# Two pairs' sums over heads and the zero words of the masks, moved from GpSimd to VectorE

## The chip, the cores and the metric

The kernel runs on one core of one Trainium2 chip. The metric is device time in microseconds (us) of the whole program. Before the change three runs gave 1026.31 (median), 1023.31 and 1027.18. The core has TensorE (matrix products), VectorE and ScalarE (elementwise work, ScalarE also the exponentials), GpSimd (elementwise work and indirect transfers), and queues from which transfers are issued; here SyncE's and GpSimd's are used. In the profile they are PE, DVE, ACT, POOL and SP. Each engine takes its instructions strictly in the order in which they were written into its queue.

## The reference

Eight batches of eight heads, 576 tokens, 64 numbers per head. Keys and values are averaged over groups of 8 tokens, so each head has 72 pooled keys. Attention over these gives one row of 512 numbers for each of 4608 tokens. Each row then goes through a mixture of eight experts:

```
logits = x @ w_gate
noisy  = logits + log1p(exp(x @ w_noise)) * noise
top2   = the two largest of the 8 noisy logits, with softmax weights
out    = sum over the two: weight * (relu(x @ w1[e]) @ w2[e])
```

with w1[e] 512x1024 and w2[e] 1024x512.

## The kernel before

**Attention.** Two batches form a pair, and there are four pairs, 0 to 3. A pair is worked through in nine chunks of 128 tokens (`ci` 0 to 8), 36 chunks in all. For each chunk TensorE transposes queries, makes scores (`qk`, lines 365 and 375), ScalarE exponentiates against a maximum from VectorE (lines 380 and 382), TensorE transposes again (`et`) and multiplies with the values (`av`, line 408). The values carry 16 more columns per head, the products of v with the two gate matrices, so that `av` also gives each head's share of the gate and noise logits. VectorE divides by the softmax sum and writes the attention rows (`xr`, line 419) and these shares (`lg`, line 421, a 128x128 product per chunk: 8 heads by 16 columns). The rows go to memory (`x_dram`).

**Routing.** `route(pr, ...)` is a generator, one for each pair. First it adds `lg` over the eight heads, in three adds that halve the number of heads each (lines 508 and 509), once for chunks 0 to 7 and once for chunk 8; in the kernel before, GpSimd does this. Line 516 on VectorE is the first reader of these sums. A chain of short VectorE and ScalarE steps on 128x72 numbers follows (softplus, the two maxima, a mask `mb` of the chosen experts at line 566). The mask has eight more columns of zeros behind its nine chunks, which the memset at line 565 writes, on GpSimd; there is one `mb` buffer for all pairs. TensorE then counts, with triangular and all-ones matrices, how many tokens chose each expert before a given one (`rk`, the rank matmuls at line 593). From rank and expert VectorE works out the place of each record (`pos`) and its words (`rec`, up to line 634).

**Record writes and the list `scq`.** Each pair has 18 record writes (9 chunks, two choices), indirect transfers on GpSimd's queue (line 637), put on a list. Behind those of pair 1 come the load of the first records of expert 0 (line 678, on GpSimd's queue) and the gathers of the first four tiles of rows (`fetch(groups[0])`, line 705, four indirect transfers on GpSimd's queue); behind pair 2's and pair 3's the same for further tiles. The program takes entries from the list a few at a time, at fixed places in each chunk: `advance(n, m)` runs `n` steps of the routing generator and then takes `m` entries. In pairs 2 and 3 a chunk takes three or four. `quiet` is 0 in chunks in which nothing is taken: in the kernel before, chunk 0 of every pair, and chunk 8 of every pair but the last. Each write also waits for an instruction of the chunk that takes it (`pace`).

**Experts.** Expert 0's tokens come in three groups. Group 0 needs only records of pairs 0 and 1, group 1 those of pairs 0 to 2, group 2 all. Stage 1 multiplies by w1 in eight blocks of 128 hidden features; each block takes twelve matmuls for a group of 512 columns (line 1016), goes into one of eight banks, and is evicted by ScalarE (`hh`, line 1027) and VectorE (`hl`, line 1028). Stage 2 multiplies by w2 (lines 1127 and 1093). Weights are split in two parts on ScalarE and VectorE (lines 480 and 481). The routing of pair 3 is driven from the first blocks of stage 1 of group 0 (`hook1`): its first sums are called in chunk 8 of pair 3, everything else after blocks 0 to 3, and the rank matmuls of pair 3 come in the program after the fourth block.

**Order.** The program's order gives priorities; a planner then writes each engine's queue from these and from its own estimates of durations, so that an instruction may stand earlier or later in its queue than the program has it.

Of the kernel before, what the change touches and what calls it, by code (L numbers as in the profile page):

```python
# [19 lines left out]
def kernel(  # L20
# [12 lines left out]
    nc = tc.nc  # L33
# [12 lines left out]
    NP = B // 2  # L46
    NCH = 9
# [286 lines left out]
    def qtr(u, half, hp=None):  # L334
        kind, pr, b, jp = u
        if half == 0:
            QTT[u] = ap_.tile([P, H, P], F32, tag="qT", name=f"qT{pr}_{b}_{jp}", bufs=2)
        elif kind == "R":
            return
        qT = QTT[u]  # L340
        qp = ps2.tile([P, 4, P], F32, tag="one", name=f"qp{pr}_{b}_{jp}_{half}", bufs=2)
        for i in range(4):
            if kind == "R":
                src = QR[pr][:, 2 * i:2 * i + 2]
            else:
                src = QT[b][:, half * 4 + i, 2 * jp:2 * jp + 2]
            nc.tensor.transpose(qp[:, i], src.rearrange("p a d -> p (a d)"), ident)  # L347
        with tc.high_priority(offset=HP if hp is None else hp):
            nc.scalar.copy(qT[:, half * 4:half * 4 + 4], qp)
# [35 lines left out]
    def et(u, jj):  # L385
        kind, pr, b, jp = u
        nm = f"{pr}_{b}_{jp}_{jj}"
        ex = EX[u][:, jj]
        eT = ap_.tile([P, NEB, P], F32, tag="eT", name=f"eT{nm}", bufs=2)
        for n0, n1 in EG:  # L390
            ep = ps2.tile([P, 512], F32, tag="one", name=f"ep{nm}_{n0}", bufs=2)
            for n in range(n0, n1):
                nc.tensor.transpose(ep[:BST, (n - n0) * P:(n - n0 + 1) * P], ex[:, ES[n]:ES[n] + BST], ident)  # L393
            with tc.high_priority(offset=HP):
                (nc.vector.tensor_copy if n0 and EV >> jj & 1 else nc.scalar.copy)(eT[:BST, n0:n1].rearrange("p n t -> p (n t)"), ep[:BST, :(n1 - n0) * P])  # L395
        return eT
# [50 lines left out]
    def wload():  # L447
        if not pieces:
            return
        e, i, h = pieces.pop(0)  # L450
        st = wp.tile([P, DF], F32, tag="wst", name=f"wst{e}_{i}_{h}", bufs=WS)
        if i < 2:
            src = moe_w1[e].rearrange("(p c) f -> p c f", p=P)[:, 2 * i + h]
            dst = st
        else:
            r0 = (i - 2) * 4 * P + h * 2 * P
            src = moe_w2[e, r0:r0 + 2 * P, :].rearrange("(c p) f -> p c f", p=P)
            dst = st.rearrange("p (c f) -> p c f", c=2)
        nc.sync.dma_start(dst, src)
        staged.append(st)  # L460
# [26 lines left out]
    def drain(g):  # L487
        for _ in g:
            pass
# [4 lines left out]
    def route(pr, c0, c1, lg, psum):  # L494
        n = c1 - c0
        k_ = [0]

        def t(*shape, dt=F32):
            k_[0] += 1
            ci = shape.index(NCH)  # L500
            r = rp.tile([P] + list(shape), dt, tag=f"rt{k_[0]}", name=f"rt{pr}_{c0}_{k_[0]}")
            return r[:, :n] if ci == 0 else r[:, :, :n]

        V = nc.vector
        L = t(NCH, 2 * E)
        for a, b in ((c0, c1 - 1), (c1 - 1, c1)):
            for h in (4, 2):
                nc.gpsimd.tensor_add(lg[:, a:b, :h], lg[:, a:b, :h], lg[:, a:b, h:2 * h])  # L508
            nc.gpsimd.tensor_add(L[:, a - c0:b - c0], lg[:, a:b, 0], lg[:, a:b, 1])
            if b < c1:  # L510
                yield
                if pr < NP - 1:
                    yield
# [48 lines left out]
            mxs.append(mx)  # L562
            ms.append(m)
        mb = rp.tile([P, NCH + 1, E], BF16, tag="mb", name=f"mb{pr}_{c0}")
        nc.gpsimd.memset(mb[:, n:], 0.0)
        V.tensor_add(mb[:, :n], ms[0], ms[1])
        rec = rp.tile([P, NCH, 2, RW], I32, tag="rec", name=f"rec{pr}_{c0}", bufs=4)

# [175 lines left out]
    def rows_of(grp, psum):  # L744
        e, t0, nt = grp
        xh = wp.tile([P, NDB, 4 * P], F32R, tag="q", name=f"xh{e}_{t0}", bufs=2)
        xl = wp.tile([P, NDB, 4 * P], F32R, tag="q", name=f"xl{e}_{t0}", bufs=2)
        XT[grp] = (xh, xl)
        for t in range(nt):
            xg = XG.pop((e, t0 + t))  # L750
            if e == 0:
                xp = psum(f"xp{t0 + t}").rearrange("p (b c) -> p b c", b=NDB)
                xv = xg.rearrange("p (c b) -> p b c", b=NDB)
                for db in range(NDB):
                    nc.tensor.transpose(xp[:, db], xv[:, db], ident)
                nr = 2 if t0 + t == 9 else 4
                xT = xp.rearrange("p b (r j) -> p b r j", j=32)[:, :, :nr]
            else:
                nr = 2 if t0 + t == 9 else 4
                xt = pools[0].tile([P, 4, NDB, 32], F32, tag="xt", name=f"xt{e}_{t0 + t}", bufs=2)  # L760
                nc.vector.transpose(xt[:, :nr], xg[:, :nr * P].rearrange("p (r i b) -> p r b i", i=32, b=NDB))
                xT = xt.rearrange("p r b j -> p b r j")[:, :, :nr]
            cs = slice(t * P, t * P + nr * 32)
            xhv = xh[:, :, cs].rearrange("p b (r j) -> p b r j", j=32)
            xlv = xl[:, :, cs].rearrange("p b (r j) -> p b r j", j=32)
            SP_[0] = (nc.scalar.copy(xhv, xT), nc.vector.tensor_sub(xlv, xT, xhv.bitcast(F32)))  # L766
            yield
# [13 lines left out]
    def advance(n, m):  # L781
        for _ in range(n):
            while gens:
                try:
                    next(gens[0])
                    break
                except StopIteration:
                    gens.pop(0)
        for _ in range(min(m, len(scq))):
            scq.pop(0)()  # L790
# [84 lines left out]
    for i, (ui, u, jj) in enumerate(chunks):  # L875
        pr, ci = divmod(i, NCH)
        if ci == 0:
            lgs[pr] = (rp if pr % 2 else ap_).tile([P, NCH, H, 2 * E], F32, tag="lg", name=f"lg{pr}")
        single = u[0] == "R"
        has = ui + 1 < NU  # L880
        if single:
            order = OR
        else:
            order = OD[jj]
        eT = None
        quiet = 0 if ci == 0 or ci == NCH - 1 and pr < NP - 1 else 1

        def bgs():
            for f in bg.get(i, ()):
                f()  # L890

        def adv():
            pace[0] = lastx[0]
            advance(STEPS[pr], 2 * quiet if pr >= NP // 2 else quiet)

        for o in order + ("" if "b" in order else "b") + ("" if "x" in order else "x"):
            if o == "v" and i == 0:
                drain(pg[0])
            if o == "b":
                bgs()  # L900
            elif o == "x":
                adv()
            elif o == "e":
                eT = et(u, jj)
            elif o == "v":
                if due:
                    due.pop()()
                if ci == NCH - 1 and pr < NP - 1:
                    gens.append(route(pr, 0, NCH, lgs[pr], one))
                elif ci == NCH - 1:  # L910
                    rt = route(pr, 0, NCH, lgs[pr], lambda nm: mone(nm))
                    next(rt)
                due.append(lambda u=u, jj=jj, ci=ci, eT=eT, lg=lgs[pr]: av(u, jj, ci, eT, lg))
            elif o in "012":
                if has:
                    qk(units[ui + 1], int(o))
                    if pr and (o == "0" or not single):
                        pace[0] = lasta[0]
                        advance(0, quiet)
            elif ui + 2 < NU:  # L920
                qtr(units[ui + 2], "qr".index(o))
        if i == 24:
            for _ in range(WS):
                wload()
        if i == 33:
            splits = rows_of(groups[0], one)
        if pr == 3 and ci:
            with tc.issue_after(lastl[0].ins), tc.issue_after(lasta[0].ins):
                next(first[0], None) if ci < 5 else next(first[1], None)
        if ci == 4 and pr >= HS:  # L930
            gens.append(route(pr, 0, 5, lgs[pr], one))
# [206 lines left out]
    def mone(name):  # L1138
        return bank()
# [174 lines left out]
```

## Time and profile before

| | |
|---|---|
| median of 3 runs | 1026.31 us |
| profiled execution, its own time | 1026.68 us |
| its span in the trace | 1024.9 us |
| PE busy | 989.9 us, 97% |
| DVE busy | 546.1 us, 53% |
| ACT busy | 343.8 us, 34% |
| POOL busy | 377.5 us, 37% |
| granted TensorE clock, mean | 0.986 of full |

The time of the profiled execution is the span plus what lies around it, 1.8 us. The page cuts the span into 40 slices of 25.6 us and gives a busy digit for each, in tenths (9 is 90% or more); PEclk is the granted clock of TensorE in the same way, where 1.00 of a window is 2.4 GHz and 0.50 is 1.2 GHz. A busy PE is not a PE at its peak. A "releaser" (after `<-`) is the instruction whose end let a waiting instruction start.

### The profile page before, as it was taken

The page shows a single profiled execution, that of the slowest core. Times are in us where ns is not written, and L with a number is a line of the kernel's source. Part 1 is how long each engine was busy: PE and PEld are TensorE (multiplying, and loading weights), DVE is VectorE, ACT ScalarE, POOL GpSimd, SP SyncE. Part 2 cuts the span into 40 slices and gives each one's busy share as a digit, 9 for nine tenths or more (in the row PEclk, how much of TensorE's full clock was granted, in tenths as well). Part 3 has the DMA queues.
Part 4 walks back from the last instruction along what each step waited for, and adds up shares of the span by engine and source line. Part 5 has one row for each costly group of instructions (what it writes and reads, how often), then busy time and mean ns, then how long its engine had stood idle before and what let it go on. Part 6 is the DMA issues. An engine that isn't in the chain of part 4 may idle for free.

```text
span 1024.9 us, 16467 instructions
## 1 busy us (share of the span) xinstructions
PE 989.9 (97%) x5832; PEld 888.6 (87%) x5832; DVE 546.1 (53%) x1261; ACT 343.8 (34%) x857; POOL 377.5 (37%) x433
## 2 busy tenths in 40 slices
PE   7999997979999999999999999999999999999996
PEld 6898896869998888898988898989888988898995
DVE  5799886583344454644464446444644455356341
ACT  4787785451213212411142124211421232123120
POOL 3023574846300442145115421551154215422514
PEclk8999998989999999999999999999999999999998
DMA  9989883344607765676267736772678358744623
GB/s 252 250 250 273 227 263 112 115 146 98 208 15 218 215 180 148 199 238 206 74 188 219 239 114 201 249 217 70 182 235 256 93 161 256 245 144 135 211 87 136
DMA packets 136006, 187.61 MB, mean 183 GB/s; under 512 B 29123, under 2 KB 84052, under 8 KB 135898
## 3 DMA queue, kind: packets, MB, share of 16 engines
q1 hardware_dynamic: 110458, 119.09, 40.5%
q0 software_dynamic: 25440, 67.05, 21.0%
q8 instruction: 72, 1.18, 0.5%
q14 instruction: 36, 0.29, 0.1%
HBM read 123.31 MB, written 70.74 MB: 189 GB/s over the span
## 4 chain that ended last, share of the span: by engine, by line
PE 87%; POOL 3%; issue 3%; ACT 2%; DMA 2%; DVE 1%; SPq 1%; POOLq 0%; ACTq 0%; DVEq 0%
PE bank L1016 37%; PE bank L1127 28%; PE bank L1093 10%; PE a L408 4%; PE s L375 2%; PE ep L393 2%; POOL rec_dram L637 1%; PE qp L347 1%; DMA v<-in_v_dram 1%; ACT ex L382 1%; ACT eT L395 1%; POOL lg L508 1%; POOL out_dram L1072 1%; PE s L365 1%; DMA rec_dram<-rec,pos 0%
## 5 line engine op out<-in xcount | busy, mean ns | idle before, releaser
L1016 PE MATMUL bank<-xh,w 128*128 128x512 f32 (+6 forms) x1536 | 391.2, 339 | 0.0
L1016 PEld LDWEIGHTS bank<-xh,w 128*128 128x128 f32 x1536 | 271.1, 189 | 20.6
L1127 PE MATMUL bank<-w,hh 128*128 128x512 f32 x880 | 271.3, 389 | 0.0
L1016 PE MATMUL bank<-xl,w 128*128 128x512 f32 (+6 forms) x768 | 260.3, 339 | 0.0
L1027 ACT ACTIVATE hh<-bank 128x512 fp32r<-128x512 f32 (+4 forms) x192 | 97.3, 508 | 460.0 <-PE bank L1016 435.7
L1028 DVE SCALAR_TENSOR_TENSOR hl<-bank,hh 128x512 fp32r<-128x512 f32 (+4 forms) x192 | 111.0, 579 | 242.2 <-ACT hh L1027 242.2
L1127 PEld LDWEIGHTS bank<-w,hh 128*128 128x128 f32 x880 | 164.9, 188 | 33.8
L1127 PE MATMUL bank<-w,hl 128*128 128x512 f32 x440 | 171.4, 389 | 0.0
L1016 PEld LDWEIGHTS bank<-xl,w 128*128 128x128 f32 x768 | 145.0, 189 | 10.4
L1064 DVE SCALAR_TENSOR_TENSOR pv<-bank,raw,pv 128x128 f32<-128x128 f32 x196 | 55.5, 342 | 109.1 <-PE bank L1127 62.4
L1068 POOL DMA_DIRECT2D slot_dram<-yt x17 | 9.8, 575 | 270.4 <-DVE yt L1064 218.4
L1093 PE MATMUL bank<-hh,w 128*128 128x240 f32 (+3 forms) x512 | 103.3, 298 | 3.1 <-ACT xh L766 1.8
L1127 PEld LDWEIGHTS bank<-w,hl 128*128 128x128 f32 x440 | 82.6, 188 | 17.2
L637 POOL DMA_INDIRECT rec_dram<-rec,pos x72 | 78.3, 1088 | 48.8 <-issue 14.2
L1048 POOL DMA_INDIRECT pv<-slot_dram,raw x70 | 68.1, 973 | 65.4 <-DMA slot_dram<-ys 33.3
L481 DVE TENSOR_TENSOR w<-wst,w 128x512 fp32r<-128x512 f32 x128 | 82.6, 681 | 10.5 <-ACT w L480 10.5
L1093 PEld LDWEIGHTS bank<-hh,w 128*128 128x128 f32 x512 | 82.5, 189 | 3.6 <-ACT xh L766 2.0
L480 ACT CAST w<-wst 128x512 fp32r<-128x512 f32 x128 | 72.8, 619 | 25.4 <-DMA wst<-in_moe_w_dram 25.2
L714 POOL DMA_INDIRECT row<-x_dram,raw x70 | 70.4, 1006 | 21.4 <-issue 19.8
L1068 POOL DMA_DIRECT2D slot_dram<-pv x55 | 31.7, 577 | 123.8 <-DVE pv L1064 97.1
L1093 PE MATMUL bank<-hl,w 128*128 128x320 f32 (+3 forms) x256 | 75.8, 296 | 0.0
L382 ACT ACTIVATE ex<-s,mx 128x72 f32<-128x72 f32 x288 | 70.6, 344 | 9.9 <-DVE mx L380 9.6
(162 smaller groups left out, 1029.6 us busy)
## 6 DMA issues: line engine op xcount, KB each, us to landing
wst<-in_moe_w_dram SPq DMA_DIRECT2D x64, 512.0 KB
via<-row SPq DMA_DIRECT2D x266, 64.0 KB
xg<-via SPq DMA_DIRECT2D x63, 256.0 KB
slot_dram<-pv POOLq DMA_DIRECT2D x55, 256.0 KB, 4.0
x_dram<-xr SPq DMA_DIRECT2D x16, 512.0 KB
q<-in_q_dram SPq DMA_DIRECT2D x7, 1024.0 KB
k<-in_k_dram SPq DMA_DIRECT2D x6, 896.0 KB
v<-in_v_dram SPq DMA_DIRECT2D x12, 432.0 KB
```

Of the source, the lines that this page charges most:

```text
L382: lasta[0] = nc.scalar.activation(ex[:, jj, EPOS[h] * G:(EPOS[h] + 1) * G], sv[:, i], AF.Exp, bias=mx[:, i:i + 1])
L480: nc.scalar.copy(hv, sv)
L481: nc.vector.tensor_sub(lv, sv, hv.bitcast(F32))
L637: s = nc.gpsimd.indirect_dma_start(out=rec_dram[:, :], out_offset=bass.IndirectOffsetOnAxis(ap=pos[:, i, c:c + 1], axis=0), in_=rec[:, c, ...
L714: turn_of("pool", lambda: nc.gpsimd.indirect_dma_start(out=row[:32 * nr], out_offset=None, in_=x_dram[:, :], in_offset=bass.IndirectOffset ...
L1016: nc.tensor.matmul(part(ph), w1s(e, a, db, f), part(xs[b][:, db]), start=(i == 0), stop=(i == 3 * NDB - 1))
L1027: act = nc.scalar.activation(hh[:, :n], ph[:, :n], AF.Relu)
L1028: last = nc.vector.scalar_tensor_tensor(hl[:, :n], ph[:, :n], 0.0, hh[:, :n].bitcast(F32), op0=OP.max, op1=OP.subtract)
L1048: turn_of("pool", lambda: nc.gpsimd.indirect_dma_start(out=pv[:np_], out_offset=None, in_=slot_dram[:P + e * CAP, :], in_offset=bass.Indir ...
L1064: nc.vector.scalar_tensor_tensor(r_, y_, wc, pv[:plain] if plain else r_, op0=OP.mult, op1=OP.add)
L1093: nc.tensor.matmul(part(py), w2s(e, b, f)[:, mb * P:(mb + 1) * P], part(hs[f][a]), start=(i == 0), stop=(i == 3 * NFB - 1))
L1127: mm = nc.tensor.matmul(py, hs[f][a][:, cs], w2s(e, b, f), start=(i == 0), stop=(i == 3 * NFB - 1))
```

## The change

The adds over heads use VectorE for pairs 2 and 3 and stay on GpSimd for pairs 0 and 1. The memset of the mask's zero words is on VectorE for all pairs. `quiet` is 1 now in chunk 8 of pair 2 and in chunk 0 of pair 3, so entries of the list are taken there too. (`NP` is 4, `NCH` is 9.)

```diff
         for a, b in ((c0, c1 - 1), (c1 - 1, c1)):
+            eng = nc.gpsimd if pr < NP // 2 else V
             for h in (4, 2):
-                nc.gpsimd.tensor_add(lg[:, a:b, :h], lg[:, a:b, :h], lg[:, a:b, h:2 * h])
-            nc.gpsimd.tensor_add(L[:, a - c0:b - c0], lg[:, a:b, 0], lg[:, a:b, 1])
+                eng.tensor_add(lg[:, a:b, :h], lg[:, a:b, :h], lg[:, a:b, h:2 * h])
+            eng.tensor_add(L[:, a - c0:b - c0], lg[:, a:b, 0], lg[:, a:b, 1])
...
         mb = rp.tile([P, NCH + 1, E], BF16, tag="mb", name=f"mb{pr}_{c0}")
-        nc.gpsimd.memset(mb[:, n:], 0.0)
+        V.memset(mb[:, n:], 0.0)
...
-        quiet = 0 if ci == 0 or ci == NCH - 1 and pr < NP - 1 else 1
+        quiet = 0 if ci == 0 and pr <= NP // 2 or ci == NCH - 1 and pr < NP // 2 else 1
```

## Rows read from the trace of the kernel before

**Rows 1.** The page: busy times; granted clock in 40 slices, in tenths.

```profile
PE 989.9 (97%) x5832; PEld 888.6 (87%) x5832; DVE 546.1 (53%) x1261; ACT 343.8 (34%) x857; POOL 377.5 (37%) x433
...
PEclk8999998989999999999999999999999999999998
```

**Rows 2.** Waits of PE: waiter, releaser, total us, times, longest us.

```profile
PE bank L593 <- DVE mb L566: 6.9, 1, 6.9
PE s L365 <- ACT ex L382: 5.9, 1, 5.9
PE kT L298 <- DVE ks L239: 2.3, 2, 1.2
```

**Rows 3.** Windows: length; PE, PEld, DVE, ACT, POOL busy (count); PEclk, DMA share, GB/s.

```profile
140.00:151.50 11.50, 11.50 (x97) 11.11 (x95) 10.31 (x22) 10.19 (x36) 9.14 (x8) 1.00 0.86 257
...
153.40:159.30 5.90, 0.02 (x2) 0.02 (x2) 1.18 (x4) 0.91 (x6) 4.15 (x7) 0.74 0.17 53
159.30:166.00 6.70, 6.70 (x37) 5.65 (x38) 3.63 (x14) 3.17 (x12) 2.96 (x4) 0.50 0.03 3
...
185.00:192.00 7.00, 6.42 (x52) 5.91 (x50) 6.64 (x16) 5.84 (x14) 5.47 (x6) 1.00 0.60 169
...
203.40:210.40 7.00, 0.07 (x3) 0.07 (x3) 5.20 (x24) 2.68 (x9) 3.29 (x7) 0.78 0.00 0
210.40:214.40 4.00, 4.00 (x19) 3.27 (x20) 4.00 (x11) 2.59 (x6) 0.70 (x2) 0.52 0.20 35
```

**Rows 4.** Timeline of POOL, end of pair 2: start, duration, instruction, [idle before <-releaser].

```profile
153.60 0.97 POOL L637 DMA_INDIRECT rec_dram<-rec,pos  x1 [0.30 <-issue]
154.59 2.06 POOL L508 TENSOR_TENSOR lg<-lg 128x512 f32<-128x512 f32 x2
```

**Rows 5.** Timeline of DVE across the turn from pair 2 to 3.

```profile
150.43 0.28 DVE L421 TENSOR_TENSOR lg<-a,rd 128x128 f32<-128x128 f32 x1
...
158.12 0.23 DVE L516 SCALAR_TENSOR_TENSOR rt<-rt 128x72 f32<-128x72 f32 x1 [6.46 <-POOL rt L509]
...
159.41 0.28 DVE L421 TENSOR_TENSOR lg<-a,rd 128x128 f32<-128x128 f32 x1
...
166.21 0.28 DVE L421 TENSOR_TENSOR lg<-a,rd 128x128 f32<-128x128 f32 x1
...
169.90 0.28 DVE L421 TENSOR_TENSOR lg<-a,rd 128x128 f32<-128x128 f32 x1
```

**Rows 6.** Timeline of DVE at the end of attention.

```profile
193.57 0.28 DVE L421 TENSOR_TENSOR lg<-a,rd 128x128 f32<-128x128 f32 x1
203.80 0.23 DVE L516 SCALAR_TENSOR_TENSOR rt<-rt 128x72 f32<-128x72 f32 x1 [9.96 <-POOL rt L509]
```

**Rows 7.** Timeline of PE at the same place.

```profile
192.28 0.48 PE L1016 MATMUL bank<-xh,w 128*128 128x512 f32 x1
...
210.36 0.23 PE L593 MATMUL bank<-mb,before 128*128 128x80 bf16 x1 [6.93 <-DVE mb L566]
```

**Rows 8.** Groups of DVE, 100 to 215 us: count, busy us, mean ns, idle before.

```profile
L481 DVE TENSOR_TENSOR w<-wst,w 128x512 fp32r<-128x512 f32 x12 | 8.0, 683 | 0.0
...
L584 DVE TENSOR_TENSOR rec<-rec,rt 128x9 f32<-128x9 f32 x3 | 0.5, 166 | 0.0
...
L1201 DVE TENSOR_TENSOR gt<-cnt,thr 128x216 f32<-128x216 f32 x1 | 0.4, 374 | 0.0
```

**Rows 9.** Timelines of DVE and POOL: an add, and a record write beside it.

```profile
146.22 1.75 DVE L233 TENSOR_TENSOR v<-v 112x1536 f32<-112x1536 f32 x1
...
147.05 1.75 POOL L637 DMA_INDIRECT rec_dram<-rec,pos  x1 [0.30 <-DMA rec_dram<-rec,pos]
```

**Rows 10.** Waits of POOL: the memset of the mask.

```profile
POOL mb L565 <- PE rk L593: 13.4, 2, 10.7
```

**Rows 11.** Timeline of POOL and the critical chain: last gather, transposes of group 2.

```profile
254.43 0.95 POOL L705 DMA_INDIRECT xg<-x_dram,raw  x1 [0.30 <-issue]
...
263.27 1.92 PE bank L755 x16
```

## The prediction, made before the result was known

> **What bounds the kernel now.** I read the page first. TensorE is busy in 97% of the span, and its granted clock is below full in three of the forty slices: the first, the seventh (about 154 to 179 us) and the ninth (205 to 231) [rows 1]. So the kernel is bound by TensorE except where it stands still, and what a change on other engines can give is the standing still and what follows from it. The list of TensorE's waits names two long ones and after them nothing above 2.3 us: 6.9 us before the rank matmuls at line 593, and 5.9 us before the score matmuls at line 365 [rows 2]. The windows put a price on each: idle from 153.4 to 159.3 and then 6.7 us at half clock (1.2 instead of 2.4 GHz) with TensorE busy throughout; idle from 203.4 to 210.4 and then 4.0 us at a mean of 0.52 [rows 3]. These are the two slow slices.
>
> Then I asked the two in-order queues what stood at their heads. The sums over heads of pair 2 stand in GpSimd's queue behind a run of record writes of pair 1: the last write starts at 153.60, the first add at 154.59 [rows 4]. VectorE's line 516, the first reader of the sums, stands idle 6.46 us for them and starts at 158.12; behind it in VectorE's queue is the softmax work of the next chunk, whose `lg` product comes only at 159.41, nearly nine microseconds after that of the chunk before (150.43) [rows 5]. That starves ScalarE's exponentials, and they starve TensorE. At the end of attention it is the same: the last chunk's `lg` is written at 193.57, but line 516 starts at 203.80, and the row says that it waited 9.96 us for GpSimd [rows 6]. The rank matmuls, six and a half microseconds of short VectorE and ScalarE steps later, come at 210.36, while TensorE, which began stage 1 at 192.28, had run out of the four hidden blocks (128 hidden features, twelve matmuls each) in front of them at 203.4 [rows 3, 7].
>
> **The change part by part.** *Sums of pairs 2 and 3 on VectorE.* Six adds per pair move: 512, 256 and 128 elements for chunks 0 to 7, and 64, 32 and 16 for chunk 8. VectorE's price for a 128x512 add of two SBUF operands is 0.68 us (line 481); 256 elements lie between the 0.37 of 216 elements and that 0.68, I take 0.42, near the row of 216; 128 elements are 0.28 (`lg` rows); 64 to 16 elements lie between 0.17 (9 elements) and 0.28, I take 0.2 each with a few hundredths between dependent steps [rows 5, 8]. First part 1.4 us, second part 0.7, together 2.1 per pair. They depend only on VectorE's own `lg` products, so nothing in front of line 516 waits for another engine any more.
>
> *First stall.* The steps from chunk to chunk by the `lg` starts are 8.98 and 6.80 us across and after the stall, and 3.69 for the next one [rows 5]. Without stall and half clock I give the two steps 3.7 each, plus the whole 2.1 of the sums, because VectorE was busy 10.31 of 11.5 us just before and offers no hole for them [rows 3]: 9.5 instead of 15.8, a gain of 6.3. The bounds: 8.4 if the sums hide, and nothing if other work fills the hole (rival C).
>
> *Second stall.* It costs 7.0 us idle and 1.9 us of the 4.0 at half clock, 8.9 in all [rows 3]. Afterwards the chain starts at the end of the last `lg` (193.85), takes up to 2.1 for the sums and the same 6.56 from line 516 to the rank matmuls [rows 6, 7]: 202.5, against TensorE's arrival at 203.4. Two more evictions of hidden blocks (0.68 each, the same shape as line 481) may be written into the chain, which makes it 203.9. So at most half a microsecond of the stall is left, and I count no half clock behind so short a wait. Against that, the first part of the sums falls into a stretch where VectorE is busy 6.64 of 7.0 us and must still split the rows that the first hidden block needs [rows 3], so the start of stage 1 slips by up to 1.4. Gain 8.9 - 1.4 - 0.5 = 7.0; bounds 8.9 and nothing.
>
> *A rule that would take some of it back.* Beside VectorE's 1.75 us add of 112x1536 at 146.22, a record write that normally takes 0.97 took 1.75, while the add kept its usual time [rows 9]. The Trainium skill (SBUF — State Buffer, SBUF: two separate sides) says that VectorE with two SBUF inputs and a GpSimd operation share one pair of ports where GpSimd reads SBUF, and that whichever starts first holds it for the whole instruction while the other is blocked. By that rule a record write in progress could also hold up each of the three large adds for up to 0.97 us, which at the end of attention would leave a stall of 2 to 3 us more, and the sum would be about 1016. The row shows only the write giving way, so I leave this out of the sum.
>
> *The zero words of the masks on VectorE.* Four memsets. The trace has none of this size on VectorE; a 9-element operation there takes 0.17 us [rows 8], which I take as the upper end, the lower end is nothing, and I count 0.1 each, 0.2 on the path. GpSimd's were beside its queue of writes and freed nothing that TensorE waited for. Where the memset stands in VectorE's order is a different matter (rival D).
>
> *Chunks no longer kept free.* Chunk 8 of pair 2 and chunk 0 of pair 3 now take items from the list: the last two record writes of pair 1, the load of its records and the four gathers of the first rows come there instead of two chunks later. These are seven or so GpSimd issues of about 1 us. They sit on GpSimd's queue alone (this load is not on SP's), what is queued behind them is no longer the sums, and the record writes of pair 2 are put on the list only in chunk 3 of pair 3. I count nothing; it is hidden under TensorE's work, and the rows are needed only at the end of attention. Each write also waits for a marker of the chunk that issues it; that wait now has only other writes behind it.
>
> *What is late next.* From the rank matmuls on, the record writes of pair 3 and the gathers of the next groups hang on the same chain as the ranks, so they come earlier by about as much as TensorE does. The tightest place: the last gather of group 2 of expert 0 starts at 254.43, TensorE transposes its rows at 263.27 [rows 11]; after some 5 us for issue and landing, 4 us of margin stay. TensorE's own list has only waits of 2.3 us or less behind the two.
>
> **Sum.** 1026.68 (the profiled execution; 1024.9 of it is the span) - 6.3 - 7.0 + 0.2 = 1013.6. The profiled execution lies 0.37 above the median of the runs, so I forecast 1013. If everything hides: 1026.3 - 8.4 - 8.9 = 1009.
>
> **Rivals.** *B, one stall stays.* The order inside each queue is written by a planner from its own estimates. If it now writes the rank matmuls ahead of some hidden blocks (after the first, TensorE would be there near 195, the ranks at 202.5), TensorE stands as long as before and only the first stall is gained: 1026.3 - 6.3 = 1020. If the first stall is replaced instead: 1019. For it: the end of attention has less than a microsecond of slack. Against it: the rank matmuls stand in the program after the fourth block, and there they stood before.
>
> *C, no change.* VectorE, nearly full before both stalls, becomes what TensorE waits for, and the 2.1 us per pair come on top of work that had moved into the hole: 1026. Against it: VectorE's and ScalarE's idle time in the first hole is idle for the sums alone, and little is pulled ahead in an in-order queue.
>
> *D, slower.* The memset of a pair's mask may not overwrite what the rank matmuls of the pair before still read. On GpSimd it stood 13.4 us for them in two of the four cases, once 10.7 [rows 10], and nobody minded. If it stands as early in VectorE's queue, VectorE stops in the middle of attention, with the maxima and products of the next chunk behind it, and TensorE runs dry as it did at 153: 13.4 us, and about 5 us for two spells of half clock [rows 3], together 18.4 against the gain of 13.3, so 1026.3 + 5.1 = 1031. It decides as soon as these waits with their clock cost exceed 13.3 us. Against it: VectorE has its own wait for the same matmuls (the running count), and a planner that puts the memset where the ranks are done would put it behind that.
>
> **How the numbers follow.** Forecast 0.68 (own range 1009 to 1017), B 0.16, C 0.06, D 0.10. A difference under 0.5%, 5.1 us, can hardly be told from none. Faster by more than that: all of the forecast and three quarters of B, 0.80. Within: the rest of B, C and two fifths of D, 0.14. Slower: the rest of D, 0.06. The range of 1009 to 1021 holds the forecast and B and leaves out C and D.
>
> **What would show it.** Right: no 5.9 and no 6.9 in TensorE's list of waits; line 516 without a wait for GpSimd in pairs 2 and 3; the granted clock full from 154 to 231; the `lg` steps around chunk 26 near 4 to 6 us; the rank matmuls within a microsecond after the fourth hidden block. Wrong: a memset of `mb` on VectorE with microseconds of idle time before it and TensorE as releaser (D); the rank matmuls after fewer than four blocks (B); hidden blocks or transposes of group 1 or 2 waiting for gathered rows.

## The result, and the profile after

The changed kernel takes 1008.55 us (median of 4 runs, 1006.87 to 1008.85), the kernel before 1026.12: a ratio of 0.983 with a 95% interval of 0.9807 to 0.9852. A later comparison on another chip gave 1008.38 against 1025.54, 0.9831 (0.981 to 0.9852). The forecast was 1013, with a range of 1009 to 1021: the direction and the mechanism were right, the gain was 17.6 us where 13.3 had been worked out, and the time lies half a microsecond below the range. The profiled execution took 1008.4 us, its span is 1006.6.

The page of the changed kernel (as rows 1):

```profile
PE 983.0 (98%) x5832; PEld 882.3 (88%) x5832; DVE 549.7 (55%) x1277; ACT 344.4 (34%) x857; POOL 370.6 (37%) x417
...
PEclk8999999999999999999999999999999999999999
```

Only the first slice is below full now. TensorE's waits, longest first (as rows 2): both long ones are gone, and nothing has taken their place.

```profile
PE kT L298 <- DVE ks L239: 2.4, 2, 1.3
PE s L375 <- ACT ex L382: 1.9, 2, 1.4
PE vTp L317 <- DVE vs L239: 1.5, 1, 1.5
```

VectorE at the turn from pair 2 to pair 3 (as rows 5; lines below 507 keep their numbers, later ones are one higher, so the adds are 509 and 510 and their first reader is 517):

```profile
144.35 0.28 DVE L421 TENSOR_TENSOR lg<-a,rd 128x128 f32<-128x128 f32 x1
145.06 0.61 DVE L380 TENSOR_REDUCE mx<-s 128x6 f32<-128x432 f32 x1 [0.43 <-PE s L375]
145.59 0.68 DVE L509 TENSOR_TENSOR lg<-lg 128x512 f32<-128x512 f32 x1
...
146.58 0.41 DVE L509 TENSOR_TENSOR lg<-lg 128x256 f32<-128x256 f32 x1
...
147.84 0.28 DVE L421 TENSOR_TENSOR lg<-a,rd 128x128 f32<-128x128 f32 x1
...
148.56 1.75 DVE L233 TENSOR_TENSOR v<-v 112x1536 f32<-112x1536 f32 x1
...
151.03 0.95 DVE L233 TENSOR_TENSOR v<-v 112x768 f32<-112x768 f32 x1
151.90 0.23 DVE L517 SCALAR_TENSOR_TENSOR rt<-rt 128x72 f32<-128x72 f32 x1
...
153.27 0.28 DVE L421 TENSOR_TENSOR lg<-a,rd 128x128 f32<-128x128 f32 x1
...
156.60 0.28 DVE L421 TENSOR_TENSOR lg<-a,rd 128x128 f32<-128x128 f32 x1
```

Line 517 waits for nobody. The three steps between the `lg` products from 144.35 to 156.60 take 12.25 us. In the kernel before the same three go from 144.98 over 150.43 and 159.41 to 166.21 [rows 5; the first is from the same view]: 21.23. So 9.0 us come from here.

```profile
144.98 0.28 DVE L421 TENSOR_TENSOR lg<-a,rd 128x128 f32<-128x128 f32 x1
```

Note the two large `v` adds (2.7 us, pooling for a later batch): before, they stood ahead of the product at 150.43 (the larger one is in rows 9); the planner has put the sums there and the `v` adds behind the product.

TensorE's own windows say what the 9.0 us consist of (columns as in rows 3). First the kernel before: the three steps one by one, then the stretch from the product of chunk 7 of pair 2 to that of the last chunk but one. Then the changed kernel: the three steps together, and the same long stretch.

```profile
144.98:150.43 5.45, 5.45 (x47) 5.31 (x47) 4.68 (x9) 4.64 (x15) 4.54 (x4) 1.00 0.90 247
150.43:159.41 8.98, 3.07 (x33) 2.47 (x33) 2.10 (x8) 2.91 (x15) 6.40 (x10) 0.82 0.45 170
159.41:166.21 6.80, 6.80 (x38) 5.75 (x39) 3.73 (x15) 3.27 (x11) 3.17 (x4) 0.50 0.03 3
144.98:190.78 45.80, 38.98 (x309) 35.12 (x309) 30.99 (x113) 30.68 (x102) 26.21 (x30) 0.89 0.50 155
```

```profile
144.35:156.60 12.25, 12.20 (x119) 11.31 (x119) 10.77 (x33) 11.05 (x39) 9.81 (x9) 1.00 0.68 233
144.35:181.12 36.77, 35.60 (x309) 32.02 (x309) 32.49 (x121) 30.83 (x102) 23.25 (x23) 1.00 0.60 192
```

The long stretch holds 309 matmuls in both. TensorE is idle in it for 1.17 us instead of 6.82, and busy with the same work for 35.60 instead of 38.98: 5.65 us of idle time and 3.4 us of half clock are gone. VectorE is busy for 1.5 us more (32.49 instead of 30.99).

The end of attention, VectorE first (as rows 6), then TensorE (as rows 7):

```profile
184.91 0.28 DVE L421 TENSOR_TENSOR lg<-a,rd 128x128 f32<-128x128 f32 x1
185.23 0.45 DVE L509 TENSOR_TENSOR lg<-lg 128x64 f32<-128x64 f32 x2
185.72 0.18 DVE L510 TENSOR_TENSOR rt<-lg 128x16 f32<-128x16 f32 x1
185.93 0.26 DVE L517 SCALAR_TENSOR_TENSOR rt<-rt 128x72 f32<-128x72 f32 x1
...
192.72 0.22 DVE L567 TENSOR_TENSOR mb<-rt,rt 128x72 bf16<-128x72 f32 x1
```

```profile
182.62 0.47 PE L1017 MATMUL bank<-xh,w 128*128 128x512 f32 x1
183.48 0.50 PE L1017 MATMUL bank<-xl,w 128*128 128x512 f32 x1 [0.39 <-DVE xl L767]
...
194.31 0.21 PE L594 MATMUL bank<-mb,before 128*128 128x80 bf16 x1
```

The mask is ready at 192.94, TensorE comes to the rank matmuls 1.4 us later and does not wait; the large adds of the sums stand between the two splits that the first block needs, and cost it a wait of 0.39. On the critical chain the transposes of group 2 start 17.76 us earlier than in rows 11:

```profile
245.51 1.92 PE bank L756 x16
```

The product of the last chunk but one stands at 181.12 where it stood at 190.78, 9.66 earlier; so the end of attention gives the other 8.1. Of the 9.66, 0.6 were there already in chunk 6 of pair 2 (140.71 against 141.34); runs of other kernels that change nothing up to there stood up to 0.95 earlier too, so I do not count it to the change.

### The profile page after: what moved, and what is told of

Read it like the earlier page. It is cut to its first block, busy times and chain, and to the rows that moved or that the text cites. A ratio compares the mean times of both kernels' runs of the same rounds, so it can differ in the third digit from the quotient of the medians.

```text
span 1006.6 us, 16461 instructions
## 1 busy us (share of the span) xinstructions
PE 983.0 (98%) x5832; PEld 882.3 (88%) x5832; DVE 549.7 (55%) x1277; ACT 344.4 (34%) x857; POOL 370.6 (37%) x417
## 4 chain that ended last, share of the span: by engine, by line
PE 90%; ACT 3%; issue 2%; DMA 2%; POOL 1%; DVE 1%; SPq 1%; POOLq 0%; ACTq 0%; DVEq 0%
PE bank L1017 39%; PE bank L1128 28%; PE bank L1094 10%; PE a L408 4%; PE s L375 3%; PE ep L393 2%; PE qp L347 1%; DMA v<-in_v_dram 1%; ACT ex L382 1%; ACT eT L395 1%; POOL out_dram L1073 1%; PE vr L325 0%; PE kT L298 0%; PE s L365 0%; POOL slot_dram L1069 0%
## 5 line engine op out<-in xcount | busy, mean ns | idle before, releaser
L481 DVE TENSOR_TENSOR w<-wst,w 128x512 fp32r<-128x512 f32 x128 | 82.7, 684 | 11.9 <-ACT w L480 11.9
```

Of the source, the lines that this page charges most:

```text
L481: nc.vector.tensor_sub(lv, sv, hv.bitcast(F32))
```

## The experiments

Eighteen runs, in the order of the questions. Each is compared with the kernel before on its own chip.

**Which pair gives what.** The sums of one pair alone on VectorE, memset and kept-free chunks as before; the edit of the kernel before, cut to the lines changed:

```diff
+            eng = V if pr == 2 else nc.gpsimd
...
-                nc.gpsimd.tensor_add(lg[:, a:b, :h], lg[:, a:b, :h], lg[:, a:b, h:2 * h])
-            nc.gpsimd.tensor_add(L[:, a - c0:b - c0], lg[:, a:b, 0], lg[:, a:b, 1])
+                eng.tensor_add(lg[:, a:b, :h], lg[:, a:b, :h], lg[:, a:b, h:2 * h])
+            eng.tensor_add(L[:, a - c0:b - c0], lg[:, a:b, 0], lg[:, a:b, 1])
```

> Only the sums of pair 2 on VectorE. Where the kernel before takes 1026 to 1028 (its two stalls are there): theory 9 us less, 1018, the 5.9 us wait gone and the 6.9 us wait left; rival (the prediction's 6.3 us) 1021. Where the kernel before takes 1048 as on two other chips (TensorE stands elsewhere and the two stalls are not there): no difference.

Measured: 1016.49 against 1026.03, ratio 0.9913 (0.9889 to 0.9936): 9.5 us less. Its waits of TensorE begin with the one that was left:

```profile
PE bank L594 <- DVE mb L567: 6.9, 1, 6.9
PE vTp L317 <- DVE vs L239: 2.7, 1, 2.7
```

And with `pr == 3`:

> Only the sums of pair 3 on VectorE. Where the kernel before takes 1026 to 1028: theory 8 us less, 1019, the 6.9 us wait gone and the 5.9 us wait left; rival (the ranks still come late while the first stall is there) 1023 or more. Where it takes 1048: no difference.

Measured: 1017.51 against 1026.03, ratio 0.9919 (0.9901 to 0.9937): 8.5 us less, and the other wait left:

```profile
PE s L365 <- ACT ex L382: 5.9, 1, 5.9
```

The two add up to 18.1 us against 17.6 of the whole. So each stall belongs to its own pair's sums, they do not hang together, and the first is worth some 9 us and not 6.3.

**Queue order or the speed of the adds.** The sums stay on GpSimd, but chunk 7 of pair 2 takes no record writes either, so four fewer stand in front of them:

```diff
-        quiet = 0 if ci == 0 or ci == NCH - 1 and pr < NP - 1 else 1
+        quiet = 0 if ci == 0 or ci == NCH - 1 and pr < NP - 1 or pr == 2 and ci == NCH - 2 else 1
```

> Kernel before with chunk 7 of pair 2 kept free of record writes too, sums on GpSimd. Where the kernel before takes 1026 to 1028: theory (the writes in front make the sums late) the first stall goes without VectorE, 1018 to 1020; rival (GpSimd's slower adds are the matter) 1025 to 1027. Where it takes 1048: no difference.

Measured: 1021.08 against 1026.03, ratio 0.9956 (0.9939 to 0.9972): 5.0 us less. That is a little over the theory's 1018 to 1020 and well under the rival's 1025 to 1027. Line 516 waits 0.82 us instead of 6.46, so the writes in front were what made the sums late, and the rival falls. But nearly half of the 9 us is missing. TensorE's row at line 365, two windows at and behind it, and the long stretch (product of chunk 7 of pair 2 to that of the last chunk but one) show where (columns as in rows 3):

```profile
153.23 0.71 PE L365 MATMUL s<-kbd,qT 64*64 64x72 f32 x14 [0.76 <-ACT ex L382]
```

```profile
153.00:154.00 1.00, 0.77 (x15) 0.69 (x16) 1.00 (x4) 1.00 (x5) 0.54 (x1) 1.00 0.09 37
154.00:161.00 7.00, 7.00 (x30) 6.04 (x31) 4.46 (x19) 3.27 (x10) 4.79 (x5) 0.51 0.13 43
144.07:184.65 40.58, 38.90 (x309) 35.06 (x309) 31.92 (x112) 30.84 (x102) 25.48 (x29) 0.92 0.51 167
```

TensorE waits 0.76 us, once, and its clock is nevertheless at 1.2 GHz from 154 to about 161, with TensorE busy all the time. Over the long stretch its idle time is 1.68 us, nearly as little as in the changed kernel (1.17), but it is busy for 38.90 us, as in the kernel before (38.98), where the changed kernel needs 35.60. So this run takes away the idle part of the stall, and the 3.3 us of half clock stay. Why the clock falls here is not shown: a longer wait at nearly the same place, in the run with extra adds below, leaves it full. The end of attention in this kernel is unchanged in kind (a wait of 8.1 us before the rank matmuls).

**The freed chunks alone**, sums and memset on GpSimd:

```diff
-        quiet = 0 if ci == 0 or ci == NCH - 1 and pr < NP - 1 else 1
+        quiet = 0 if ci == 0 and pr <= NP // 2 or ci == NCH - 1 and pr < NP // 2 else 1
```

> Only the chunks freed for record writes, sums and memset on GpSimd. Where the kernel before takes 1026 to 1028: theory (queue order on GpSimd makes the sums late) the first stall grows by 1.3 to 8 us, 1028 to 1035; rival (the freed chunks count nothing whoever does the sums) 1026 to 1027. Where the kernel before takes 1048: no difference.

Measured: 1030.0 against 1025.54, ratio 1.0038 (1.0021 to 1.0055): slower, as the queue order has it. GpSimd's timeline shows the sums of chunk 8 behind the load and the four gathers, and the list of TensorE's waits a stall of 12.7 us:

```profile
155.85 0.96 POOL L637 DMA_INDIRECT rec_dram<-rec,pos  x1 [0.30 <-issue]
156.83 2.07 POOL L508 TENSOR_TENSOR lg<-lg 128x512 f32<-128x512 f32 x2
...
165.62 0.96 POOL L705 DMA_INDIRECT xg<-x_dram,raw  x1 [0.31 <-issue]
166.60 0.66 POOL L508 TENSOR_TENSOR lg<-lg 128x64 f32<-128x64 f32 x2
```

```profile
PE ep L393 <- ACT qT L349: 13.4, 3, 12.7
```

**The same edits taken back one at a time from the changed kernel.** First the chunks kept free as before:

> Changed kernel with chunk 8 of pair 2 and chunk 0 of pair 3 kept free of record writes as before. Theory (freeing them counts nothing once the sums are off GpSimd): 1008 to 1009. Rival (the freed chunks gave the 2 to 3 us by which the first stall's gain exceeded the forecast): 1011.

Measured: 1008.19 against 1027.76 (0.9813, 0.9791 to 0.9834). Then the memset on GpSimd as before:

> Changed kernel with the zero words of the masks written by GpSimd as before. Theory (the memset counts nothing on either engine): 1008 to 1009. Rival (on GpSimd it waits at the head of the queue for the rank matmuls and holds up the record writes behind it): 1010 or more.

Measured: 1008.38 (0.9811, 0.9795 to 0.9827). Both theories hold: without the sums on GpSimd's queue neither edit is worth anything that can be measured, and keeping the chunks free was only the price of having the sums there.

**Is VectorE full at the first stall?** The six adds of pair 2 twice more, into a scratch tile:

```diff
+        scr = ap_.tile([P, NCH, 4, 2 * E], F32, tag="scr", name=f"scr{pr}") if pr == 2 else None
...
+            for _ in range(2 if pr == 2 else 0):
+                for h in (4, 2, 1):
+                    eng.tensor_add(scr[:, a:b, :h], lg[:, a:b, :h], lg[:, a:b, h:2 * h])
```

> Changed kernel with the six adds of pair 2 done three times over on VectorE, the extra two sets into a scratch tile (2 x 1.9 us of VectorE's time at the place of the first stall). Theory (VectorE is not what the chunks wait for there, so the prediction was wrong to charge the adds in full): at most 1.5 us slower, 1008 to 1010. Rival (VectorE has no hole there, as the prediction had it): 3.9 us slower, 1012 to 1013.

Measured: 1010.9 (1009.32 to 1011.18) where the changed kernel and its two neighbours above take 1008.2 to 1008.6: about 2.5 us slower, between the theory and the rival. The `lg` products say the same:

```profile
144.50 0.28 DVE L421 TENSOR_TENSOR lg<-a,rd 128x128 f32<-128x128 f32 x1
...
159.17 0.28 DVE L421 TENSOR_TENSOR lg<-a,rd 128x128 f32<-128x128 f32 x1
...
187.31 0.28 DVE L421 TENSOR_TENSOR lg<-a,rd 128x128 f32<-128x128 f32 x1
```

These stand 0.15, 2.57 and 2.40 us later than in the changed kernel. TensorE's idle time says the same: in the long stretch it is 3.56 us (39.14 less 35.58) where the changed kernel has 1.17, 2.4 more.

```profile
144.50:183.64 39.14, 35.58 (x309) 31.89 (x309) 35.36 (x133) 30.96 (x102) 24.28 (x22) 1.00 0.55 180
```

The 3.9 us of the expectation are a sum of durations, and in the timelines an instruction starts before the one ahead of it has ended. VectorE's busy time grows by 2.9 us (35.36 against 32.49), and of these 2.4 reach the path: for further adds VectorE has hardly a hole. This price does not carry over to the first set, the sums themselves, which make VectorE busy for 1.5 us more than in the kernel before: with these alone TensorE waits only 0.05 of the 12.25 us of the three steps.

The run also bears on the clock. TensorE waits longer here than in the run with chunk 7 kept free, and its clock stays full:

```profile
155.25 0.43 PE L393 MATMUL ep<-ident,ex 128*112 128x128 f32 x2 [1.05 <-ACT ex L382]
```

```profile
154.00:163.00 9.00, 6.61 (x60) 5.39 (x58) 8.85 (x38) 6.94 (x23) 4.92 (x6) 1.00 0.19 68
```

**Sums of all pairs on VectorE**, and nothing kept free (`eng = V`, `quiet = 1`):

> Changed kernel with the sums of all four pairs on VectorE and no chunk kept free of record writes. Theory (pairs 0 and 1 lost nothing to their sums but a wait of about half a microsecond each, and VectorE's 2 us per pair are partly hidden): 1006 to 1010. Rival (VectorE is full in pairs 1 and 2, where it also pools the keys and values): 1011 to 1013.

Measured: 1008.81 (1007.81 to 1012.48; 0.9824, 0.9798 to 0.9851): the same as the changed kernel. No version here beats it.

**Taking the clock's part away at the second stall.** In the kernel before, TensorE is given 40 transposes ahead of the rank matmuls of pair 3:

```diff
+        for i in range(40 if pr == NP - 1 else 0):
+            nc.tensor.transpose(rk[:, i % 4 * P:(i % 4 + 1) * P], ident, ident)
```

> Kernel before with 40 transposes of the identity on TensorE ahead of the rank matmuls of pair 3, into the bank that these overwrite: TensorE works through the second stall instead of idling, and the chain is as late as before. Theory (the half clock after a stall is a price of its own, 1.9 us here): 1024 where the kernel before takes 1026, and full clock from 203 on. Rival (the 4.0 us after the stall are slow for another reason, the evictions or the weight splits): 1026, with the clock full and the matmuls no faster.

Measured: 1030.36 against 1025.54, ratio 1.0051 (1.0035 to 1.0068): slower, which neither theory had. The transposes were done in 4.5 us and left a wait:

```profile
201.24 4.53 PE L593 MATMUL bank<-ident 128*128 128x128 f32 x40
208.26 0.21 PE L595 MATMUL bank<-mb,before 128*128 128x80 bf16 x1 [2.49 <-DVE mb L566]
```

The clock still fell (0.59 and 0.55 from 209 to 213). And something else came late, on the critical chain the loads of the weight pieces for stage 2:

```profile
224.00:230.00 6.00, 3.36 (x12) 1.59 (x10) 5.28 (x12) 3.16 (x6) 4.65 (x5) 0.99 0.79 184
```

Here TensorE was busy 3.4 of 6.0 us. Why the planner's new order brings the weights later I did not follow up; the run says nothing about the clock.

**Two chips on which the stalls are not there.** The first four runs fell on a chip on which the kernel before takes 1048.05 us (31 runs, 1039.58 to 1054.67), and a repeat on a second such chip (1048.27).

> Only the sums of pair 2 on VectorE; pair 3's sums, the masks' zero words and the kept-free chunks as before. Theory: each stall is lost by its own pair's sums, and the first is worth 9.0 us (the lg products after it stand 9.0 us earlier in the changed kernel): 1017, the 5.9 us wait gone, the 6.9 us wait there. Rival (what the prediction had for it, 6.3 us, is the sums' part, and the rest came from the freed chunks or the memset): 1020. Second rival (the two stalls hang together): below 1014 or above 1023.

Measured: 1054.07, ratio 1.0048 (1.0019 to 1.0077); the repeat:

> Only the sums of pair 2 on VectorE, once more, on a chip on which the kernel before shows its two stalls. Theory: the first stall alone goes, 9 us by the traces: 1.5 us either side of 1018 where the kernel before takes 1027, with the 6.9 us wait before the rank matmuls still there. Rival (the prediction's 6.3 us is the sums' part): 1021.

1052.42, ratio 1.0043 (1.0007 to 1.0078).

> Only the sums of pair 3 on VectorE; all else as before. Theory: the stall at the end of attention alone goes, 8.1 us by the traces: 1018, with the 5.9 us wait at line 365 still there. Rival (the sums' own time eats part of it, as the prediction had it): 1019. They differ by less than the runs tell apart; what counts is whether this and the run with pair 2 alone add up to the 17.6 us of the whole change.

Measured: 1045.78, ratio 0.9978 (0.9951 to 1.0006); the repeat:

> Only the sums of pair 3 on VectorE, once more. Theory: the stall at the end of attention alone goes, 8 us: 1019 where the kernel before takes 1027, with the 5.9 us wait at line 365 still there. Rival (the two hang together: with the first stall left, the ranks still come late): 1023 or more.

1047.95, ratio 0.999 (0.9953 to 1.0027).

> Only the chunks are freed for record writes; all sums and the memset stay on GpSimd. Theory (GpSimd's queue order is what makes the sums late): in pair 2 the sums now stand behind one to four more record writes of 1.3 us each and perhaps the load and the gathers, so the first stall grows by 1.3 to 8 us: 1028 to 1035. Rival (the freed chunks count nothing whoever does the sums): 1026.

Measured: 1053.83, ratio 1.0051 (1.0021 to 1.008); the repeat:

> Only the chunks freed for record writes, sums and memset on GpSimd, once more. Theory (queue order on GpSimd makes the sums late): the first stall grows by 1.3 to 8 us, 1028 to 1035 where the kernel before takes 1027. Rival (the freed chunks count nothing whoever does the sums): 1027.

1050.44, ratio 1.0024 (0.999 to 1.0059).

> Kernel before with one more chunk kept free of record writes (chunk 7 of pair 2, beside its chunk 8); the sums stay on GpSimd. Theory (the sums were late because of the writes in front of them, not because GpSimd adds slowly): four writes less stand before them, GpSimd has caught up when chunk 7's product is there, and the first stall goes without VectorE: 1017 to 1019. Rival (GpSimd's 4 us for the six adds are the matter, against 2 on VectorE): 1024 to 1026, with most of the 5.9 us wait left.

Measured: 1049.65, ratio 0.9994 (0.9958 to 1.0031); the repeat:

> Kernel before with chunk 7 of pair 2 kept free of record writes too, sums on GpSimd, once more. Theory (the writes in front make the sums late): the first stall goes without VectorE, 1018 to 1020 where the kernel before takes 1027. Rival (GpSimd's slower adds are the matter, 2 us of them at most): 1025 to 1027.

1048.61, ratio 1.0003 (0.9969 to 1.0036). None of these tells the theories apart, because TensorE stands elsewhere there. With pair 2's sums on VectorE on the first of these chips its longest waits are

```profile
PE xp L756 <- issue: 7.5, 1, 7.5
PE ep L393 <- ACT qT L349: 7.1, 5, 3.7
```

"Issue" is waiting for nothing that the profile shows. The chunks go by more slowly (the first and the last `lg` product stand at 26.9 and 215.1 us in that run, at 29.9 and 193.6 in the kernel before on a chip of the first kind), and the 6.9 us wait is not in the list although pair 3's sums are as before. With pair 3's sums alone moved the 5.9 us wait is not there either, and line 517 waits only 1.4 us in all for GpSimd's sums. From the kernel before itself no trace of such a chip is kept. What makes these chips slow, why pair 2's sums on VectorE cost about half a per cent there, and what the whole change does there, stay open: it did not come to run on one.

> The changed kernel beside the two above. Where the kernel before takes 1026 to 1028: 1008 to 1009. Where it takes 1048, with neither of the two stalls: theory (the change takes away these two stalls and nothing else) 1046 to 1050; rival (it also relieves what is slow there) 1040 or less.

This one ran on a chip of the first kind, with the 1008.38 given at the top.

## Why the prediction was right and where it was wrong

*The two stalls and their cause: right.* Both are gone, each with its own pair's sums (9.5 and 8.5 us alone), and keeping four more writes from GpSimd's queue takes most of the first wait away without VectorE.

*First stall, 6.3 us: the term that was mis-sized; it measured 9.0.* The step that failed is "I give the two steps 3.7 each, plus the whole 2.1 of the sums, because VectorE was busy 10.31 of 11.5 us just before and offers no hole for them". It sizes TensorE's loss by the distance of VectorE's products, and TensorE's own windows show both of its terms too large. In the kernel before TensorE was busy 3.07 us in the first of the two steps and 6.80 at half clock in the second, by an estimate 3.07 + 3.40 = 6.5 at full clock, not 7.4: 0.9 us. With the step ahead of them (5.45, TensorE busy throughout) the three steps needed 11.9 us of TensorE; with the sums on VectorE they take 12.25, so the sums cost 0.3 and not 2.1: 1.8 us. Together these are the 2.7 us that were missing. Part of the 2.1 came from adding up durations that overlap (VectorE's busy time grew by 1.5). For the rest, VectorE was as busy as the rows said, but that did not make it what TensorE waits for: in the changed kernel it is busy 10.77 of the 12.25 us, and TensorE is idle for 0.05.

The second stall was priced by idle time and half clock. The same from rows 3 would have given 5.9 + 3.35 = 9.25 for the first, close to what was measured. "8.4 if the sums hide" was no bound, since it holds the same 7.4, and with it the low end of the range fell.

*Second stall, 7.0: measured 8.1.* Its price of 8.9 was nearly right. The 6.9 us wait is gone, and from the rank matmuls to the transposes of group 2 the program now takes 51.20 us instead of 52.91, so 8.6 us of the stall and its half clock are gone. The 1.4 us by which the first blocks were to slip measured 0.5 (11.69 us from the first matmul of stage 1 to the rank matmuls, where the four blocks took 11.15), and the half microsecond of rest was nothing. The planner put the large adds between the two splits instead of ahead of both, which cost a wait of 0.39, and the chain (7.0 us from line 517 to the end of the mask, one eviction more than before) still ended 1.4 us ahead of TensorE. No half clock came behind that short wait, as the prediction had it: the clock is full in every slice but the first.

*A misreading without effect.* Four of the forty slices of rows 1 are below full, not three; the last one is the fourth. It lies at the end of the program, and the forecast does not use it.

*The rule of the Trainium skill (SBUF — State Buffer, SBUF: two separate sides) that I left out: rightly.* The sums' large adds took 0.68 to 0.73 and 0.41 to 0.48 us beside record writes, close to their price, and those writes kept their 0.96 to 0.97. Beside the long `v` add it was again the write that gave way; this one normally takes 0.97 and stood beside the `v` add at 148.56, which kept its 1.75:

```profile
148.96 2.32 POOL L638 DMA_INDIRECT rec_dram<-rec,pos  x1 [0.30 <-DVE mx L380]
```

*Memset and rival D: nothing.* The four memsets take 0.06 us each and none has idle time before it, where 0.2 us had been counted for them. With the memset back on GpSimd the time is the same.

*Freed chunks: nothing, as counted,* but only because the sums had left GpSimd; alone they cost 4.5 us.

*Rivals B and C did not happen:* the rank matmuls still come after four blocks, and no long wait for VectorE has come into TensorE's list in place of the two.

## What to carry to other kernels

A short chain that the next stage waits for does not belong on an in-order queue that also issues a long run of transfers: its place in that queue, more than the engine's speed, set when it ran, and keeping slots free around it only bought back part. Size a stall on the engine that limits the time: its idle time, plus what the same work loses at half clock behind it. The distance between another engine's products is a poor measure, since a planner moves them while the limiting engine stands where it stood. A nearly full engine can still take more work without cost, as long as the limiting engine does not wait for it; giving it more of the same work shows when the hole is used up, not what the first piece costs.

## What I had not expected of the hardware

The clock behind a short wait. In the kernel with chunk 7 kept free TensorE lacked 0.76 us of work between 152 and 154 and then ran at 1.2 GHz for nearly seven microseconds, as long as behind the 5.9 us stall of the kernel before (6.7 us at 0.50, rows 3). Yet in the run with the extra adds a wait of 1.05 us left the clock full. So the length of the wait alone does not decide; what does, these runs do not show.

Two adds with both operands in SBUF, one on GpSimd and one on VectorE, lengthened each other, while of an add and a record write only the write gave way: in that same kernel GpSimd's first two adds took 2.69 us together instead of 2.06 [rows 4], and the `v` add beside them 1.93 instead of 0.95.

```profile
147.92 2.69 POOL L508 TENSOR_TENSOR lg<-lg 128x512 f32<-128x512 f32 x2
...
148.09 1.93 DVE L233 TENSOR_TENSOR v<-v 112x768 f32<-112x768 f32 x1
```

It is not always both: in the kernel before GpSimd's two adds of pair 1 took 2.68 us at 106.56, and the `v` add of the same size at 107.68 took 0.97. Taking the sums of pairs 2 and 3 off GpSimd takes such meetings away there; what that is worth was not measured.
